# Score matmuls reordered in the diagonal sets, and the last full-array matmul ahead of a score phase issued in three parts

## The chip, the core and the metric

The kernel runs on one NeuronCore of one Trainium2 chip. The metric is the device time of one execution in microseconds. Five engines run side by side, each with its own instruction stream: TensorE (PE, which multiplies matrices; its weight loads are shown as a row of their own, PEld), VectorE (DVE), ScalarE (ACT), GpSimd (POOL) and SyncE (SP, which issues DMAs). They wait for each other through semaphores.

## What is computed

Four blocks follow one another on a 2048x512 input in bf16, each after a layer norm and with a residual: A, B, A, B. Block A is attention with 32 heads of 16 dimensions in four segments of 512 tokens, with a causal softmax inside a segment and a linear memory of the segments before. Block B is linear attention.

```python
def _A_ref(x, wq, wk, wv, wo, beta):
    ...
    for s in range(N):
        qs, ks, vs = (q[:, :, s].copy(), k[:, :, s].copy(), v[:, :, s].copy())
        logits = jnp.einsum('bhqd,bhkd->bhqk', qs, ks) * scale + mask
        p = _softmax(logits, axis=-1)
        a_dot = jnp.einsum('bhqk,bhkd->bhqd', p, vs)
        pq = phi(qs)
        num = jnp.einsum('bhld,bhde->bhle', pq, M)
        den = jnp.einsum('bhld,bhd->bhl', pq, z)[..., None] + 1e-06
        a_mem = num / den
        o = g * a_mem + (1.0 - g) * a_dot
        ...
x = A_x
x = x + _A_ref(_layernorm(x, axis=-1), A_wq, A_wk, A_wv, A_wo, A_beta)
x = x + _B_ref(_layernorm(x, axis=-1), B_wqkv, B_w_phi, B_wo)
x = x + _A_ref(_layernorm(x, axis=-1), A_wq, A_wk, A_wv, A_wo, A_beta)
x = x + _B_ref(_layernorm(x, axis=-1), B_wqkv, B_w_phi, B_wo)
```

## The kernel before

All weights and the residual stream X stay in SBUF. The kernel first records every operation of the program as an object (`Op`), with its engine, what it reads and writes, and for PE the list of its matmuls (`op.mms`: pairs of a function that gives the operands, and a number of columns). Four long tables of numbers, found beforehand, then fix everything that a scheduler would decide: `ORDER` is the order of the operations (a negative number is a filler of matmuls on zeros, an operation named "idle"; a number over 10000 is a mate, below), and others give the engine of an operation that several could run and the buffers. `finalize` works out the semaphore waits and emits each engine's instructions in that order. The tables are the same before and after.

Most of PE's work uses the whole array: 128 rows of contraction by 128 columns of weights. These are the projections (256 moving columns for K and V of block A, 512 for the output projections and for block B, 128 for the queries of A), the products of probabilities and values (17 columns each, one set of weights each), and the small products of the linear attentions. They are called full matmuls below.

The scores of block A are different. A head has only 16 dimensions, and a pair of heads fills 32 rows, so a score matmul uses one of four row groups of the array. An operation named "score" (made in `a_att`) holds the matmuls of two row groups, a = 2y and 2y + 1, for y = 0 or 1, and fills two PSUM banks (1024 columns), on which one ACT instruction then takes the exponential (`PT<-PS`, 128x1024). Three such bank pairs exist; a score operation waits until the exponential that used its pair before has read it. Where `ORDER` says so, the operations of y = 0 and y = 1 are mates: their matmuls are issued in turn, two of one and two of the other, so that all four row groups are used. A stretch of score matmuls between full ones is called a score phase.

There are two kinds of score sets. Off the diagonal, all matmuls of a set have the same 128 or 256 columns. A diagonal set has two blocks on the diagonal and one block under it: for each diagonal block two matmuls of 64 columns with the weights KP and four with the weights K, then for the block under it two of 128 columns with K. That makes 14 matmuls, the 128-column ones last, and there are 128 such operations in the program. Each matmul has its own weight load.

A PE operation without a mate is emitted by one line of `finalize`, which calls the operation's own `emit`: a loop over `op.mms` that calls `matmul`, and the semaphore is counted up by the last of them.

Of the kernel before, what the change touches and what calls it, by code (L numbers as in the profile page):

```python
# [275 lines left out]
class Program:  # L276
# [134 lines left out]
    def finalize(self, block, n_dma=40):  # L411
        nc, ops = self.nc, self.ops
        esem = {e: nc.alloc_semaphore(f"tk_{e}") for e in COMPUTE}
        dsem = [nc.alloc_semaphore(f"dma{i}") for i in range(n_dma)]
        for e in COMPUTE:
            for k, i in enumerate(x for x in self.queues[e] if not ops[x].isdma):
                ops[i].sem, ops[i].tick = ("e", e), k + 1
        q = self.queues["pool"]
        for a, b in zip(q, q[1:]):
            if ops[a].alone or ops[b].alone:  # L420
                ops[b].need.add(a)
        used = [0] * n_dma
        last = [None] * n_dma
        k = 0
        start_order = sorted((o for o in ops if o.isdma), key=lambda o: (o.done, o.i))
        for o in start_order:
            s = k % n_dma
            k += 1
            if last[s] is not None:
                o.need.add(last[s])  # L430
            last[s] = o.i
            used[s] += 16
            o.sem, o.tick = ("d", s), used[s]
        n_waits = {e: 0 for e in ENGS}
        state = {e: {} for e in ENGS}
        plan = {e: [] for e in ENGS}
        pos = {e: 0 for e in ENGS}
        clock = {}
        left = sum(len(q) for q in self.queues.values())
        while left:  # L440
            moved = False
            for e in ENGS:
                q = self.queues[e]
                while pos[e] < len(q):
                    op = ops[q[pos[e]]]
                    if any(x not in clock for x in op.need):
                        break
                    st = state[e]
                    want = {}
                    for x in op.need:  # L450
                        o = ops[x]
                        if e == "pe" and o.sem == ("e", "pe"):
                            continue
                        if want.get(o.sem, (0, None))[0] < o.tick:
                            want[o.sem] = (o.tick, x)
                    waits = []
                    for sem, (v, x) in sorted(want.items(), key=lambda kv: -clock_size(clock, kv[1][1])):
                        if st.get(sem, 0) >= v:
                            continue
                        waits.append((sem, v))  # L460
                        for s2, v2 in clock[x].items():
                            if st.get(s2, 0) < v2:
                                st[s2] = v2
                    n_waits[e] += len(waits)
                    mine = dict(st)
                    mine[op.sem] = max(mine.get(op.sem, 0), op.tick)
                    if e == "pe":
                        st[op.sem] = op.tick
                    clock[op.i] = mine
                    plan[e].append((waits, op))  # L470
                    pos[e] += 1
                    left -= 1
                    moved = True
            assert moved, "the order of the queues has a cycle"
        sec = {"sp": block.sync, "pe": block.tensor, "act": block.scalar, "dve": block.vector, "pool": block.gpsimd}
        obj = lambda s: esem[s[1]] if s[0] == "e" else dsem[s[1]]
        finals = [(("d", s), used[s]) for s in range(n_dma) if used[s]]
        for e in ENGS:
            def body(eng, e=e):
                beside, bare = None, e == "act"  # L480
                for waits, op in plan[e]:
                    if bare and not op.isdma:
                        eng.preload_act_table_set("natural_log_exp_and_others")
                        bare = False
                    for sem, v in waits:
                        eng.wait_ge(obj(sem), v)
                    if op is beside:
                        continue
                    beside = op.mate
                    if beside is None:  # L490
                        ins = op.emit[e](eng)
                        ins.then_inc(obj(op.sem), 16 if op.isdma else 1)
                        continue
                    lag = max(0, len(op.mms) - len(beside.mms))
                    for k in range(0, lag + len(beside.mms), 2):
                        for o, k0 in ((op, k), (beside, k - lag)):
                            for f in o.mms[max(0, k0):max(0, k0 + 2)]:
                                ins = matmul(eng, f)
                                if f is o.mms[-1]:
                                    ins.then_inc(obj(o.sem), 1)  # L500
                if e == "sp":
                    for sem, v in finals:
                        if state["sp"].get(sem, 0) < v:
                            eng.wait_ge(obj(sem), v)
            sec[e](body)
        self.n_waits = n_waits
        self.plan = plan
# [6 lines left out]
def clock_size(clock, x):  # L514
    return sum(clock[x].values())


def matmul(e, f):
    o, l, r, st, sp = f[0]()
    return e.matmul(o, l, r, start=st, stop=sp, tile_position=(basep(l), basep(o)))  # L520


def basep(ap):
    st = ap.ap[0][0]
    return int(ap.offset) // int(st) if st else 0
# [14 lines left out]
class Kernel:  # L540
# [10 lines left out]
    def pe(self, mms, reads, writes, pre=(), lat=0.2, cost=None, rows=0, name="", mode=0):  # L551

        def emit(e):
            for f in mms:
                ins = matmul(e, f)
            return ins
        if cost is None:
            cost = sum(mm_cost(f[1]) for f in mms)
        op = self.P.add("pe", emit, cost, reads, writes, lat=lat, pre=pre, name=name)
        op.weight = min(1.0, sum(f[1] for f in mms) * 0.000417 / cost)  # L560
        op.mode, op.rows, op.mms = int(rows > 0), rows, mms
        return op
# [471 lines left out]
    def a_att(self, s, tss, seg, AM, starts, ends, done, by_pe=()):  # L1034
# [12 lines left out]
        o = {}  # L1047
# [3 lines left out]
        def strip(a, par, g, j):  # L1051
            return K.ap[32 * a:32 * a + 32, par, g, j * 128:(j + 1) * 128]

        def both(a, g, j):
            return seg["KP"][j].ap[32 * a:32 * a + 32, g, :]

        for n, unit in enumerate(units):
# [20 lines left out]
            for y, pt in enumerate(pts):  # L1078
                P.pri = at(ts, n + 0.5 * y)
                st = self.PS.tile("st")  # L1080
                mms, reads = [], []

                def put(left, item, q, c, m, y=y, st=st):
                    qt = QT[q // 256]
                    for b in range(2):
                        def f(a=2 * y + b, b=b):
                            x = st.slot[b] * 512 + c * 64
                            return (self.ps[:, x:x + m], left(a), qt.ap[32 * a:32 * a + 32, item[1], q % 256:q % 256 + m], True, True)
                        mms.append((f, m // 4))
                for item, off in zip(unit, offs):  # L1090
                    g = item[1]
                    if item[0] == "S":
                        par, j, qs = item[2:]
                        reads += [K((par, j)), K((par, j, 1)), K(("both", j))] + [QT[i // 2](i % 2) for i in qs]
                        put(lambda a, par=par, g=g, j=j: strip(a, par, g, j), item, qs[0] * 128, off, 128 * len(qs))
                    else:
                        i = item[2]
                        reads += [K((1, i)), K((0, i)), K((1, i, 1)), K(("both", i)), seg["KP"][i](), QT[i // 2](i % 2)]
                        put(lambda a, g=g, i=i: both(a, g, i), item, i * 128, off, 64)
                        for par in range(2):  # L1100
                            put(lambda a, par=par, g=g, i=i: strip(a, par, g, i), item, i * 128 + 64, 6 + off // 4 if par else off + 1, 64)
                op = self.pe(mms, reads, [st()], pre=[pt], lat=0.23, cost=0.23, rows=y + 1, name="score")
                op.place = (self.L, s, n)
                self.act(lambda e, st=st, pt=pt: e.activation(  # L1104
# [9 lines left out]
            for ts in tss:  # L1114
                for g in range(NG):
# [7 lines left out]
                    for a in range(4):  # L1123
                        mms, used = [], []
# [351 lines left out]
```

## Time and profile before

| | us |
|---|---|
| median of 3 runs | 479.1 |
| lowest and highest of them | 478.38, 481.18 |
| the profiled execution, its own time | 478.63 |
| span of the profiled execution, first to last instruction | 476.9 |
| PE busy in the span | 465.2 |
| ACT busy | 429.7 |
| DVE busy | 424.0 |
| POOL busy | 268.9 |

The granted TensorE clock was 1.000 over the whole span. The time beside the span, 478.63 - 476.9 = 1.7 us, is start and end of the execution. A busy time sums the records of an engine without their overlaps. The end of a matmul's record is modelled, and lies some 0.17 us behind the point from which the next matmul can start, so that PE's busy share says little. What matters for PE is the distance from one matmul's start to the next one's start, which the timeline shows to 0.01 us. In a row of the timeline, the first number is the start, the second the time from there to the end of the last record in the group, and "x4" the number of instructions merged into the row.

### The profile page before, as it was taken

What the parts mean: (1) busy time and instruction counts of PE and PEld (TensorE: products, weight loads), DVE (VectorE), ACT (ScalarE), POOL (GpSimd) and SP (SyncE); (2) the same over time, 40 slices, a digit from 0 to 9 for tenths busy, and PEclk for the clock granted to TensorE, in tenths of its full rate; (3) what the DMA queues carried; (4) which work ended last, traced back from release to release, by engine and by line L of the source; (5) the groups of instructions that cost most, each with busy time, mean ns of one, the idle gap of its engine ahead of it and who ended that gap; (6) DMA issues with size and microseconds to landing.
All of it is one profiled execution on the core that took longest, in us unless ns stands there. A gap on an engine that the chain in (4) does not pass through costs nothing.

```text
span 476.9 us, 19206 instructions
## 1 busy us (share of the span) xinstructions
PE 465.2 (98%) x8309; PEld 319.3 (67%) x8309; DVE 424.0 (89%) x1008; ACT 429.7 (90%) x666; POOL 268.9 (56%) x435
## 2 busy tenths in 40 slices
PE   7999999999999999999999999999999999999997
PEld 6786677567756567557687666766765666665763
DVE  6999899989998988688999999999998888978885
ACT  3989999999999999986799899989999999999742
POOL 3686758656756685510267575784677578761100
DMA  8679661342422132320346417155434121313366
GB/s 264 115 202 147 144 92 25 69 69 47 48 46 47 25 65 51 36 55 4 67 62 97 74 21 134 25 75 83 59 63 63 25 47 33 51 38 58 70 128 186
DMA packets 115091, 35.86 MB, mean 75 GB/s; under 512 B 106816, under 2 KB 115008, under 8 KB 115008
## 3 DMA queue, kind: packets, MB, share of 16 engines
q1 hardware_dynamic: 112608, 32.54, 38.3%
q10 hardware_dynamic: 2400, 2.11, 1.4%
q8 instruction: 65, 1.06, 0.9%
q14 instruction: 18, 0.15, 0.1%
HBM read 6.32 MB, written 2.10 MB: 18 GB/s over the span
## 4 chain that ended last, share of the span: by engine, by line
PE 59%; DVE 18%; ACT 17%; DMA 3%; POOL 2%; issue 1%; POOLq 0%; DVEq 0%
PE PS L520 57%; ACT PT L1104 12%; DVE D L1110 2%; DVE stats L801 2%; DVE Vt L1228 2%; ACT Ek L1200 2%; DVE xn L817 1%; PE PS L601 1%; DMA EQ<-xn 1%; PE PS L1431 1%; DMA OT<-O 1%; DVE O L1139 1%; ACT K L1285 1%; DVE X L1165 1%; DVE Zk L1209 1%
## 5 line engine op out<-in xcount | busy, mean ns | idle before, releaser
L1104 ACT ACTIVATE PT<-PS 128x1024 bf16<-128x1024 f32 x288 | 284.6, 1083 | 7.8 <-PE PS L520 7.5
L1110 POOL TENSOR_TENSOR D<-PT,modd 128x256 bf16<-128x256 bf16 x133 | 91.6, 699 | 54.2 <-ACT PT L1104 39.1
L1113 POOL TENSOR_SCALAR_AFFINE_SELECT PT<-PT 128x512 bf16<-128x512 bf16 x128 | 83.9, 664 | 30.8 <-DVE D L1110 27.4
L520 PEld LDWEIGHTS PS<-VT,PT 128*128 128x128 bf16 x2048 | 75.0, 96 | 19.2 <-POOL PT L1113 2.5
L520 PE MATMUL PS<-VT,PT 128*128 128x17 bf16 x2048 | 82.4, 171 | 0.7 <-POOL PT L1113 0.2
L520 PE MATMUL PS<-QT,K 32*128 32x64 bf16 (+2 forms) x2176 | 77.9, 213 | 0.3
L520 PE MATMUL PS<-VT,D 128*128 128x17 bf16 x512 | 59.9, 170 | 0.0
L520 PEld LDWEIGHTS PS<-QT,K 32*128 32x128 bf16 x2176 | 41.5, 93 | 20.6 <-ACT PT L1104 10.5
L1110 DVE TENSOR_TENSOR D<-PT,modd 128x256 bf16<-128x256 bf16 x123 | 42.9, 362 | 2.9 <-ACT PT L1104 1.5
L520 PEld LDWEIGHTS PS<-VT,D 128*128 128x128 bf16 x512 | 43.2, 96 | 0.0
L1228 DVE TENSOR_TENSOR Vt<-PS,Zk 128x1024 bf16<-128x1024 f32 (+1 forms) x34 | 39.0, 1158 | 2.0 <-PE PS L520 1.0
L801 DVE BATCH_NORM_STATS2 stats<-X 128x6 f32<-128x512 bf16 x56 | 37.3, 681 | 2.5 <-DMA X<-in_A_x_dram 2.2
L1200 ACT ACTIVATE Ek<-PS 128x512 bf16<-128x512 f32 x64 | 37.6, 664 | 0.9 <-PE PS L520 0.9
L520 PE MATMUL PS<-WA_v,xA 128*128 128x256 bf16 x256 | 36.6, 273 | 0.1
L520 PE MATMUL PS<-WA_k,xA 128*128 128x256 bf16 x256 | 36.3, 273 | 0.2 <-POOL xA L907 0.2
L520 PE MATMUL PS<-xA,WA_q 128*128 128x128 bf16 x512 | 35.7, 219 | 0.5 <-DVE MS L986 0.2
L1165 DVE TENSOR_TENSOR X<-X,PS 128x512 bf16<-128x512 bf16 x50 | 33.7, 679 | 2.2 <-PE PS L520 1.8
L1207 POOL TENSOR_TENSOR Vt<-Ek 128x512 f32<-128x512 bf16 x24 | 27.9, 1164 | 12.9 <-ACT Ek L1200 10.4
L520 PEld LDWEIGHTS PS<-xA,WA_q 128*128 128x128 bf16 x512 | 29.8, 98 | 4.6 <-issue 0.6
L520 PE MATMUL PS<-WA_o,OT 128*128 128x512 bf16 x128 | 32.0, 380 | 0.6 <-DMA OT<-O 0.4
L520 PE MATMUL PS<-WB_o,OT 128*128 128x512 bf16 x128 | 32.1, 379 | 0.1
L1304 POOL COPY O<-rho 128x512 bf16<-128x512 bf16 x24 | 14.9, 634 | 26.5 <-DVE rho L1297 23.3
(157 smaller groups left out, 980.7 us busy)
## 6 DMA issues: line engine op xcount, KB each, us to landing
X<-in_A_x_dram SPq DMA_DIRECT2D x3, 512.0 KB, 9.9
EQ<-in_B_wqkv_dram SPq DMA_DIRECT2D x2, 512.0 KB, 5.4
out_dram<-X SPq DMA_DIRECT2D x8, 128.0 KB, 2.0
out_dram<-X ACTq DMA_DIRECT2D x8, 128.0 KB, 1.9
OT<-O SPq DMA_TRANSPOSE x42, 3.2
WB_v<-in_B_wqkv_dram SPq DMA_DIRECT2D x1, 512.0 KB, 4.3
WA_o<-in_A_wo_dram SPq DMA_DIRECT2D x1, 512.0 KB, 6.5
WB_o<-in_B_wo_dram SPq DMA_DIRECT2D x1, 512.0 KB, 4.7
```

Source lines behind the costliest of these rows:

```text
L520: return e.matmul(o, l, r, start=st, stop=sp, tile_position=(basep(l), basep(o)))
L601: ins = e.transpose(self.bank(gen).bitcast(BF16)[:, dt * 128:(dt + 1) * 128], src()[:, dt * 128:(dt + 1) * 128], self.ident[:])
L801: self.dve(lambda e, t=t, src=src: e.bn_stats(self.stats[:, t, :], src()), 0.603, [held() if held else R("X", t)], [R("stats", t)], name=" ...
L817: self.dve(lambda e, t=t, n=n, xn=xn: e.tensor_scalar(xn.ap[:, n], self.X[:, t, :], self.mv[:, t, 0:1], self.rstd[:, t:t + 1], op0=ALU.sub ...
L1104: self.act(lambda e, st=st, pt=pt: e.activation(pt.ap[:].rearrange("p b c -> p (b c)"), self.ps[:, st.slot[0] * 512:st.slot[0] * 512 + 102 ...
L1110: self.either(lambda e, d=d, k=k, pt=pt: e.tensor_tensor(d.ap[:, :, k, :].rearrange("p b (z c) -> p b z c", z=2), self.ends(pt.ap[:, :, 25 ...
L1113: self.pool(lambda e, q=quarters: e.affine_select(q(), q(), [[0, 4], [1, 128]], ALU.is_ge, 0.0, base=0, channel_multiplier=-1), 0.6, [pt() ...
L1165: self.dve(lambda e: e.tensor_tensor(X[:, t, :], X[:, t, :], self.bank(gen), ALU.add), 0.6, [R("X", t), gen()], [R("X", t)], name="resid")
L1200: self.act(lambda e, sgn=sgn, Ek=Ek, gen=gen: e.activation(Ek.ap[:, sgn, :], self.bank(gen), ACT.Exp, scale=1.0 - 2.0 * sgn), 512, [gen()] ...
L1207: self.pool(lambda e, Ek=Ek, sums=sums: e.tensor_tensor(sums(), *(Ek.ap[:].rearrange("p s (h j) -> p s h j", h=H)[:, :, :, 8 * k:8 * k + 8 ...
L1228: self.dve(lambda e, w=w, n=n, Vt=Vt, Zk=Zk, gen2=gen2: e.tensor_tensor(self.signed(Vt)[:, w, :, 0:16], self.bank(gen2).rearrange("p (h d) ...
L1304: P.add(("act", "pool"), {"act": lambda e, dst=dst, src=src: e.activation(dst(), src(), ACT.Copy), "pool": lambda e, dst=dst, src=src: e.t ...
```

## The change

The change has two parts. In `a_att`, the matmuls of a score operation are sorted by their columns, the widest first (the sort is stable). Sets off the diagonal stay as they are; in a diagonal set the two matmuls of 128 columns now come first. In `finalize`, the operation that follows on the same engine is looked up. Where PE's next operation is a score operation and the present one is a plain operation whose last matmul has at least 256 columns, that last matmul is issued as three: the first half of the columns, then a quarter, then a quarter, all with the same weights, and the third counts up the semaphore.

```diff
-                for waits, op in plan[e]:
+                for (waits, op), follow in zip(plan[e], plan[e][1:] + [(None, None)]):
...
                     if beside is None:
-                        ins = op.emit[e](eng)
+                        if follow[1] is not None and e == "pe" and follow[1].name == "score" and op.mms and op.name != "idle" and op.mms[-1][1] >= 256:
+                            for f in op.mms[:-1]:
+                                matmul(eng, f)
+                            ins = in_parts(eng, op.mms[-1])
+                        else:
+                            ins = op.emit[e](eng)
                         ins.then_inc(obj(op.sem), 16 if op.isdma else 1)
                         continue
...
+def in_parts(e, f):
+    o, l, r, st, sp = f[0]()
+    n, m = o.shape[1], r.shape[1]
+    for a, b in ((0, 2), (2, 3), (3, 4)):
+        ins = e.matmul(o[:, n * a // 4:n * b // 4], l, r[:, m * a // 4:m * b // 4], start=st, stop=sp and b == 4, tile_position=(basep(l), basep(o)))
+    return ins
...
                             put(lambda a, par=par, g=g, i=i: strip(a, par, g, i), item, i * 128 + 64, 6 + off // 4 if par else off + 1, 64)
+                mms.sort(key=lambda m: -m[1])
                 op = self.pe(mms, reads, [st()], pre=[pt], lat=0.23, cost=0.23, rows=y + 1, name="score")
```

In the whole program 81 full matmuls are divided: 38 of 256 columns (into 128, 64 and 64) and 43 of 512 columns (into 256, 128 and 128). PE's matmuls go from 8309 to 8471, 162 more, with 162 more weight loads. No other engine's instructions change, nor do the waits.

The next two lists show PE in the first layer, at about 155 to 157 us of the span: four matmuls of block B's value projection (`WB_v,xB`), a diagonal score operation alone, two matmuls of block B's query projection (`EQ,WB_q`), and another diagonal score operation. First before:

```order
L520 MATMUL PS<-WB_v,xB 128x512 x4
L520 MATMUL PS<-QT,KP 128x64 x2
L520 MATMUL PS<-QT,K 128x64 x4
L520 MATMUL PS<-QT,KP 128x64 x2
L520 MATMUL PS<-QT,K 128x64 x4
L520 MATMUL PS<-QT,K 128x128 x2
L520 MATMUL PS<-EQ,WB_q 128x512 x2
```

And with the change:

```order
L525 MATMUL PS<-WB_v,xB 128x512 x3
L532 MATMUL PS<-WB_v,xB 128x256
L532 MATMUL PS<-WB_v,xB 128x128 x2
L525 MATMUL PS<-QT,K 128x128 x2
L525 MATMUL PS<-QT,KP 128x64 x2
L525 MATMUL PS<-QT,K 128x64 x4
L525 MATMUL PS<-QT,KP 128x64 x2
L525 MATMUL PS<-QT,K 128x64 x4
L525 MATMUL PS<-EQ,WB_q 128x512
L532 MATMUL PS<-EQ,WB_q 128x256
L532 MATMUL PS<-EQ,WB_q 128x128 x2
```

The fourth `WB_v` matmul and the second `EQ,WB_q` matmul became three each, and the pair of 128 columns moved from the end of the score phase to its beginning.

The same for a last matmul of 256 columns, at about 14 us: four matmuls of the key projection (`WA_k,xA`), then two diagonal score operations that are mates. Before:

```order
L520 MATMUL PS<-WA_k,xA 128x256 x4
L520 MATMUL PS<-QT,KP 128x64 x4
L520 MATMUL PS<-QT,K 128x64 x8
L520 MATMUL PS<-QT,KP 128x64 x4
L520 MATMUL PS<-QT,K 128x64 x8
L520 MATMUL PS<-QT,K 128x128 x4
```

With the change:

```order
L525 MATMUL PS<-WA_k,xA 128x256 x3
L532 MATMUL PS<-WA_k,xA 128x128
L532 MATMUL PS<-WA_k,xA 128x64 x2
L525 MATMUL PS<-QT,K 128x128 x4
L525 MATMUL PS<-QT,KP 128x64 x4
L525 MATMUL PS<-QT,K 128x64 x8
L525 MATMUL PS<-QT,KP 128x64 x4
L525 MATMUL PS<-QT,K 128x64 x8
```

Here the fourth `WA_k` matmul became one of 128 and two of 64 columns, and the four 128-column score matmuls moved ahead of the 24 of 64 columns.

## The prediction

> **What bounds the kernel now.** I read the page first, then the windows, then the timeline of PE around score phases. The page's span, PE line and chain:
>
> ```profile
> span 476.9 us, 19206 instructions
> PE 465.2 (98%) x8309; PEld 319.3 (67%) x8309; DVE 424.0 (89%) x1008; ACT 429.7 (90%) x666; POOL 268.9 (56%) x435
> PE 59%; DVE 18%; ACT 17%; DMA 3%; POOL 2%; issue 1%; POOLq 0%; DVEq 0%
> PE PS L520 57%; ACT PT L1104 12%; DVE D L1110 2%; DVE stats L801 2%; DVE Vt L1228 2%; ACT Ek L1200 2%; DVE xn L817 1%; PE PS L601 1%; DMA EQ<-xn 1%; PE PS L1431 1%; DMA OT<-O 1%; DVE O L1139 1%; ACT K L1285 1%; DVE X L1165 1%; DVE Zk L1209 1%
> ```
>
> The chain that ended last runs through PE for 59% of the span, 57% of it line 520, the line that issues every matmul the change touches. ACT's exponential (L1104) has 12%. The windows show that this holds through the middle of the program (PE busy is the third number, then PEld, DVE, ACT, POOL and the granted clock), and the waits what the weight loader is held by most:
>
> ```profile
> 120.00:240.00 120.00, 118.43 (x2053) 78.24 (x2051) 104.62 (x245) 109.25 (x186) 58.12 (x92) 1.00 0.26 44
> 240.00:360.00 120.00, 119.18 (x2336) 85.78 (x2335) 114.84 (x287) 113.95 (x151) 79.70 (x126) 1.00 0.45 71
> PEld PS L520 <- ACT PT L1104: 22.0, 68, 0.6
> ```
>
> PE is hardly ever empty, and the clock is full. So a nanosecond more or less between two matmuls counts for between 0.57 of itself (the chain's share) and all of it. The next rows give matmuls and loads of each width, grouped:
>
> ```profile
> L520 PE MATMUL PS<-VT,PT 128*128 128x17 bf16 x2048 | 82.4, 171 | 0.7 <-POOL PT L1113 0.2 <-DVE VT L737 0.2
> L520 PE MATMUL PS<-WA_k,xA 128*128 128x256 bf16 x256 | 36.3, 273 | 0.2 <-POOL xA L907 0.2
> L520 PE MATMUL PS<-xA,WA_q 128*128 128x128 bf16 x512 | 35.7, 219 | 0.5 <-DVE MS L986 0.2 <-DVE X L1165 0.2
> L520 PE MATMUL PS<-WA_o,OT 128*128 128x512 bf16 x128 | 32.0, 380 | 0.6 <-DMA OT<-O 0.4 <-DVE Vt L1228 0.2
> L520 PEld LDWEIGHTS PS<-VT,PT 128*128 128x128 bf16 x2048 | 75.0, 96 | 19.2 <-POOL PT L1113 2.5 <-issue 2.3 <-ACT PT L1104 1.9
> ```
>
> The second number behind the bar is the record of one: 171 ns at 17 columns, 219 at 128, 273 at 256, 380 at 512. Most of it overlaps the next matmul. The distance from start to start follows from timeline rows with a run of equal matmuls, as (length of the row minus one record) over (count minus 1):
>
> ```profile
> 179.83 1.90 PE L520 MATMUL PS<-WA_o,OT 128*128 128x512 bf16 x8
> 54.12 1.05 PE L520 MATMUL PS<-WA_k,xA 128*128 128x256 bf16 x8
> 99.50 0.55 PE L520 MATMUL PS<-xA,WA_q 128*128 128x128 bf16 x7
> 182.42 0.27 PE L520 MATMUL PS<-VT,PT 128*128 128x17 bf16 x5
> ```
>
> For 512 columns (1.90 - 0.380) / 7 = 0.217 us, for 256 (1.05 - 0.273) / 7 = 0.111, for 128 (0.55 - 0.219) / 6 = 0.055, for 17 (0.27 - 0.171) / 4 = 0.025. From 256 to 512 columns it grows by 0.106, so a column takes 0.414 ns: 0.212, 0.106, 0.053 and 0.007 us of streaming. On top come 0.002 to 0.005 us a matmul for the wide ones and 0.018 for 17 columns.
>
> **The switches.** Around score phases PE loses more. These rows show six score phases (`QT,K` and `QT,KP`), with what comes ahead of them or the first full matmul behind:
>
> ```profile
> 182.54 0.17 PE L520 MATMUL PS<-VT,D 128*128 128x17 bf16 x1
> 182.65 0.40 PE L520 MATMUL PS<-QT,K 32*128 32x128 bf16 x16
> 182.98 0.29 PE L520 MATMUL PS<-Vt,Ek 128*128 128x136 bf16 x2
> ...
> 99.98 0.40 PE L520 MATMUL PS<-QT,K 32*128 32x256 bf16 x8
> ...
> 155.14 1.02 PE L520 MATMUL PS<-WB_v,xB 128*128 128x512 bf16 x4
> 156.09 0.20 PE L520 MATMUL PS<-QT,KP 32*128 32x64 bf16 x2
> ...
> 156.43 0.60 PE L520 MATMUL PS<-EQ,WB_q 128*128 128x512 bf16 x2
> 156.97 0.20 PE L520 MATMUL PS<-QT,KP 32*128 32x64 bf16 x2
> ...
> 13.77 0.61 PE L520 MATMUL PS<-WA_k,xA 128*128 128x256 bf16 x4
> 14.31 0.21 PE L520 MATMUL PS<-QT,KP 32*128 32x64 bf16 x4
> 14.35 0.23 PE L520 MATMUL PS<-QT,K 32*128 32x64 bf16 x8
> 14.41 0.20 PE L520 MATMUL PS<-QT,KP 32*128 32x64 bf16 x4
> 14.44 0.28 PE L520 MATMUL PS<-QT,K 32*128 32x64 bf16 x12
> 14.65 0.28 PE L520 MATMUL PS<-WA_v,xA 128*128 128x256 bf16 x1
> ...
> 152.37 0.39 PE L520 MATMUL PS<-QT,K 32*128 32x256 bf16 x4
> 152.69 0.39 PE L520 MATMUL PS<-WB_k,xB 128*128 128x512 bf16 x1
> ```
>
> The time from the end of the last full matmul's streaming to the first score matmul is: behind 17 columns 0.11 - 0.007 = 0.10 us; behind 128 columns, with the run of seven from 99.50 to 99.98, 0.48 - 6 x 0.055 - 0.053 = 0.10; behind 512 columns 0.95 - 3 x 0.217 - 0.212 = 0.09, and at 156.43 0.54 - 0.217 - 0.212 = 0.11; behind 256 columns 0.54 - 3 x 0.111 - 0.106 = 0.10. It is one figure, whatever the width of the last matmul. The first score matmul had 64, 128 or 256 columns in these rows, which makes no difference either.
>
> **Part 1, the last full matmul in three.** It removes 81 matmuls and adds 243. Per division of 512 columns: 0.111 + 2 x 0.055 - 0.217 = 0.004 us. Per division of 256: one of 128 and two of 64 columns. A full matmul of 64 columns stands nowhere in this trace; its streaming is 0.0265, and the part on top lies between the 0.002 of 128 columns and the 0.018 of 17. I take 0.003, because four score matmuls of 64 columns that run side by side, with four loads, come at 0.03 (14.35 to 14.41 is two rounds). That makes 0.055 + 2 x 0.0295 - 0.111, or 0.003; since two matmuls more cost twice what stands on top, I use 0.005 for either kind: 81 x 0.005 = 0.4 us more. At the upper end, with 0.018, a division of 256 costs 0.055 + 2 x 0.0445 - 0.111 = 0.033, in all 38 x 0.033 + 43 x 0.005 = 1.5 us. At the lower end the switch behind a narrow part is shorter than read by the scatter of these readings, 0.02: 81 x 0.02 = 1.6 us less.
>
> The weights of the added parts are loaded again, 162 times, at 0.096 us a record. I cost that at nothing: the 17-column matmuls each bring their own load of the same 128 x 128 and follow each other at 0.025 us, so such a load is hidden behind the matmuls ahead of it even where these are narrow.
>
> Against this stands a rule of the Trainium skill, TensorE: Matmul & The Clock Gate, Part 3, "The mechanism": a weight load overlaps matmuls in flight only where their row groups differ. A full matmul fills all row groups, so by that rule each added load would be exposed, an estimate of 162 x 0.096 = 15.6 us; the 0.025 us of the 17-column rows does not agree with it for full matmuls that follow one another, while a load for a score matmul behind a full one does behave so.
>
> **Part 2, the widest score matmuls first.** No instruction is added. In a score phase the time from first start to the next full matmul is 0.32 us for two rounds of 256 columns (152.37), 0.33 for four of 128 (182.65), 0.34 for the diagonal one of six rounds of 64 and one of 128 (14.31). Each holds 512 columns for every row group, 0.212 us; the rest is 0.11, 0.12 and 0.13, about 0.004 for each round more. A diagonal set has seven rounds in either order, and the way out costs the same behind 128 and behind 256 columns. So I take 0. Behind a last round of 64 columns no row shows it; the bound is one step of these three, 0.01 us to either side, times some 100 diagonal phases (128 operations, part of them mates): 1.0 us less or more. The semaphores still count up behind the last matmul of each operation, so no exponential starts earlier or later than by these nanoseconds, and nothing is queued behind a new wait.
>
> **The sum** is 0.4 us on PE, of which 0.57 to 1.0 reaches the end: 0.3. The profiled execution took 478.63, so it would take 478.9; the median of the runs shown is 479.1, so I forecast 479.4. With the bounds of both parts, -2.6 us at 0.57 and +2.5 in full, the forecast's own range is 477.6 to 481.6.
>
> **Rivals.** *The added loads are exposed because the parts are short (slower).* This takes a load that can hide only behind the one matmul ahead. A part of 64 columns streams for 0.0265 us, one of 128 for 0.053, one of 256 for 0.106; a load of 0.096 would stick out by 0.043 behind 128 columns and 0.070 behind 64. In a division of 256 both later loads and the next would pay: the second part 0.043, the third 0.070; of 512 only the third, 0.043. Sum 38 x 0.113 + 43 x 0.043 = 6.2 us, 3.5 to 6.2 at the end, so 482.6 to 485.3. It decides from 0.03 us a division (2.4 / 81). For it speaks only the record's length, against it the 0.025. Chance 0.22, with 0.03 of it for no overlap at all.
>
> *The switch becomes shorter (faster).* The way into a score phase costs 0.10 us, 81 times 8.1 us. If the loads of the first score matmuls may start once only a short last part is in the array, half of it might go: 4.0 - 0.4 = 3.6 us less, 475.5. It decides from 0.035 us a switch. Against it: 0.10 behind 17 columns as behind 512. For it: no row has a last matmul with the same weights as the one ahead. Chance 0.22.
>
> *The change meets PE while it waits anyway.* Where the loader waits for the exponential (68 times, 22.0 us), the added nanoseconds vanish: then the time stays at 479.1. Chance 0.12.
>
> **The numbers.** The forecast has 0.44. About 0.5%, 2.4 us, is what a measurement of this kernel can tell from no change. The forecast and the third rival lie within it: same 0.56, faster 0.22, slower 0.22. The range takes in the faster rival and the lower end of the slower one: 475.0 to 483.0.
>
> **What would show it.** Right: start to start 0.03 us for the 64-column parts and 0.055 for those of 128; the step from the last part to the score phase at 0.09 to 0.11 behind its streaming; 0.34 from a diagonal phase's start to the next full matmul. Wrong: a step into the score phase under 0.07, parts over 0.06 at 64 columns, or a diagonal phase that is more than 0.01 from 0.34.

## The result, and the profile after

| | before | after |
|---|---|---|
| median of 20 runs, us | 478.87 | 481.75 |
| lowest and highest | 478.04, 481.18 | 479.86, 484.5 |
| ratio, with its 95% interval | | 1.0062 (1.0052 to 1.0073) |
| profiled execution and its span | 478.63, 476.9 | 481.51, 478.7 |

The change made the kernel slower by 0.6%, 2.9 us. The page of the changed kernel, its head, the instruction queue and the chain:

```profile
span 478.7 us, 19530 instructions
PE 466.8 (98%) x8471; PEld 336.5 (70%) x8471; DVE 422.8 (88%) x1008; ACT 430.1 (90%) x666; POOL 268.0 (56%) x435
q8 instruction: 66, 1.08, 1.0%
PE PS L525 53%; ACT PT L1118 13%; DMA OT<-O 5%; ACT Ek L1214 2%; PE PS L532 2%; DVE stats L814 2%; DVE Vt L1242 2%; DMA X<-in_A_x_dram 1%; DVE D L1124 1%; PE PS L614 1%; PE PS L1445 1%; DVE O L1153 1%; DVE xn L830 1%; ACT K L1299 1%; DVE O L1356 1%
```

Two things differ from before. The transposing DMA of the attention output (`OT<-O`) went from 1% of the chain to 5%, though no DMA was touched. And the queue q8, which brings instructions, has 66 packets where it had 65:

```profile
q8 instruction: 65, 1.06, 0.9%
```

The two profiled executions differ by 2.9 us, but their spans by 1.8 only. The time beside the span went from 1.7 to 2.8 us, and the trace of the changed kernel has one more instruction packet, 1.8 us behind the last instruction (DMA view of 478.7 to 482 us):

```profile
q8 instruction: 1, 0.02, 2.4%
```

The kernel before has no packet there. In the 83 further executions of it on record the time beside the span is 1.7 to 1.8 us; in 8 of the 20 of the changed kernel it is 1.9 to 2.8. The only other trace below with such a late packet (64 instructions more, kernel before) is the only other one with over 1.8 us beside the span. That the end waits for this packet is argued from this coincidence. It is not the whole loss, since the median span is 480.0 us in the changed kernel against 477.0 before; the profiled execution, with 478.7, is one of the shorter ones, and its trace shows only a part of the usual loss.

The place that the prediction worked out, in the timeline of the changed kernel (columns: start, length, group; "x3" in line 532 is the divided matmul):

```profile
155.43 0.81 PE L525 MATMUL PS<-WB_v,xB 128*128 128x512 bf16 x3
156.07 0.38 PE L532 MATMUL PS<-WB_v,xB 128*128 128x256 bf16 x3
156.39 0.23 PE L525 MATMUL PS<-QT,K 32*128 32x128 bf16 x2
...
156.73 0.39 PE L525 MATMUL PS<-EQ,WB_q 128*128 128x512 bf16 x1
156.95 0.38 PE L532 MATMUL PS<-EQ,WB_q 128*128 128x256 bf16 x3
157.27 0.23 PE L525 MATMUL PS<-QT,K 32*128 32x128 bf16 x2
```

From the first `WB_v` matmul to the score phase it is 0.96 us (before 0.95), from `EQ,WB_q` to the next one 0.54 (before 0.54), and the diagonal phase between them takes 0.34 (before 0.34). Over all sites, the median time from the start of the last full matmul, or of its first part, to the first score matmul went from 205 to 210 ns (38 of 256 columns) and from 311 to 316 ns (43 of 512). That is 0.005 us a site, 0.4 us in all. So the two edits cost nothing that could be 2.9 us where they stand.

The time is lost elsewhere. The waits of PE for the transpose `OT<-O` (total, times, longest), before:

```profile
PE PS L520 <- DMA OT<-O: 0.4, 1, 0.4
```

and after:

```profile
PE PS L525 <- DMA OT<-O: 1.9, 4, 0.7
```

One of the four places is at 137 us. Before, the output projection `WA_o,OT` follows the last probability product at once:

```profile
137.53 0.17 PE L520 MATMUL PS<-VT,D 128*128 128x17 bf16 x1
137.55 1.02 PE L520 MATMUL PS<-WA_o,OT 128*128 128x512 bf16 x4
```

With the change PE stands there:

```profile
137.39 0.17 PE L525 MATMUL PS<-VT,D 128*128 128x17 bf16 x1
137.84 0.81 PE L525 MATMUL PS<-WA_o,OT 128*128 128x512 bf16 x3 [0.28 <-DMA OT<-O]
```

PE arrived 0.14 us earlier than before and left 0.29 us later. The transpose was not issued later: SyncE started it at 133.04 us before and at 132.95 after. It took longer. The DMA view of 132.5 to 136.5 us, before:

```profile
q1 hardware_dynamic: 1761, 0.44, 58.2%
issues: line engine op xcount, KB each, median us to landing
OT<-O SPq DMA_TRANSPOSE x1, 3.2
K<-ktok SPq DMA_TRANSPOSE x1, 3.1
```

and after:

```profile
q1 hardware_dynamic: 1559, 0.39, 95.3%
q8 instruction: 1, 0.02, 1.7%
issues: line engine op xcount, KB each, median us to landing
OT<-O SPq DMA_TRANSPOSE x1, 4.8
K<-ktok SPq DMA_TRANSPOSE x1, 4.3
```

An instruction packet lies in the window now, and both transposes in flight landed 1.2 to 1.6 us later. The packets of q8 are 16 KB. PE has 8309 matmuls and as many weight loads, 16,618 instructions, and 65 packets: 256 instructions a packet, and counted in the trace PE works off 255 instructions on average between one packet's start and the next one's (157 to 356). So q8 is read as PE's own instruction stream. It adds up over the run: of the 100 transposes, those with a q8 packet running between 1.2 and 3.2 us after their issue landed after 4.08 us on average before (42 of them) and 4.08 after (43), the others after 3.22 (58) and 3.23 (57). It is no strict rule: of the 36 that landed later than 3.6 us in the changed kernel, called late below, 29 met such a packet and 7 did not. But it holds in all fourteen traces of this document, with means of 3.8 to 4.2 us against 3.2 to 3.3, and it is not that some transposes are slow by themselves. The transposes are the same 100 in every kernel, and 94 of them landed at least twice with such a packet and twice without; in 93 of the 94 the mean with the packet is the later one, by 0.8 us on average. In the changed kernel about as many are met as before, but others: of its 36 late ones, 20 were late before as well.

The theory is therefore this. The 162 added matmuls and their loads are 324 instructions, 1.3 packets, spread over the program. They move each later fetch against the transposes, and the order of the kernel happens to suit the old places of the fetches better than the new ones. These places, against the transposes, are called the phase of the fetches. The rivals: the added instructions cost time by their number, the parts cost it by standing ahead of a score phase, or the sort costs it.

### The profile page after: what moved, and what is told of

It reads as the page before. It is cut to its first block, busy times and chain, and to the rows that moved or that the text cites. A ratio compares the mean times of both kernels' runs of the same rounds, so it can differ in the third digit from the quotient of the medians.

```text
span 478.7 us, 19530 instructions
## 1 busy us (share of the span) xinstructions
PE 466.8 (98%) x8471; PEld 336.5 (70%) x8471; DVE 422.8 (88%) x1008; ACT 430.1 (90%) x666; POOL 268.0 (56%) x435
## 4 chain that ended last, share of the span: by engine, by line
PE 57%; ACT 18%; DVE 15%; DMA 7%; POOL 1%; issue 1%; ACTq 0%; POOLq 0%; DVEq 0%
PE PS L525 53%; ACT PT L1118 13%; DMA OT<-O 5%; ACT Ek L1214 2%; PE PS L532 2%; DVE stats L814 2%; DVE Vt L1242 2%; DMA X<-in_A_x_dram 1%; DVE D L1124 1%; PE PS L614 1%; PE PS L1445 1%; DVE O L1153 1%; DVE xn L830 1%; ACT K L1299 1%; DVE O L1356 1%
## 5 line engine op out<-in xcount | busy, mean ns | idle before, releaser
L525 PE MATMUL PS<-QT,K 32*128 32x128 bf16 (+2 forms) x2176 | 81.1, 214 | 1.2 <-ACT PT L1118 0.2
L525 PEld LDWEIGHTS PS<-QT,K 32*128 32x128 bf16 x2176 | 45.5, 93 | 18.3 <-ACT PT L1118 3.1
L525 PE MATMUL PS<-WA_v,xA 128*128 128x256 bf16 x236 | 34.4, 273 | 0.1
L525 PE MATMUL PS<-WA_k,xA 128*128 128x256 bf16 x238 | 34.4, 274 | 0.2 <-POOL xA L920 0.2
L525 PE MATMUL PS<-WA_o,OT 128*128 128x512 bf16 x117 | 29.6, 380 | 1.0 <-DMA OT<-O 1.0
```

## Experiments, one part of the change at a time

All ratios are against the kernel before, on the same chip.

**The sort alone.** The line `mms.sort(key=lambda m: -m[1])` is put into the kernel before.

> Only the order of the score matmuls in the diagonal sets is changed; nothing is divided. Three theories of the 2.9 us. Number: the 162 added matmuls and loads cost it through what PE has to be supplied with, wherever they stand. Place: the parts cost it because they stand right ahead of a score phase. Sort: the widest-first order costs it. Number and place both expect this kernel within 0.3 us of before (478.9); sort expects about 481.3, that is 2.4 us more.

Measured: 478.68 us, ratio 1.000 (0.9989 to 1.0012). The sort costs nothing, and its theory falls. This kernel has as many instructions at each place as the one before.

**The parts alone.**

```diff
-                mms.sort(key=lambda m: -m[1])
```

> Only the last full matmul ahead of a score phase is issued in three parts; the score matmuls keep their old order. Number and place both expect about 481.5 (2.4 to 2.9 us more than before). Sort expects 0.4 us more than before, the direct cost of 81 divisions at 0.005 us.

Measured: 481.84 us, 1.0055 (1.0036 to 1.0075). The whole loss comes with the parts.

**Two halves, without the sort.**

```diff
-    for a, b in ((0, 2), (2, 3), (3, 4)):
+    for a, b in ((0, 2), (2, 4)):
```

> Parts alone, but two halves instead of a half and two quarters: 81 matmuls and loads are added, not 162. Number expects half of the cost of the three parts, 1.2 to 1.5 us more than before. Place expects nearly all of it where a divided matmul as such disturbs the score phase, or none where the small size of the last part does. Sort expects 0.2 us more.

Measured: 478.26 us, 0.9993 (0.9983 to 1.0003). Half of the added instructions cost nothing at all, which number does not explain.

**The same parts elsewhere, without the sort.** 38 of the 90 matmuls of 256 columns and 43 of the 212 of 512 columns that end an operation with no score operation behind it, evenly spread:

```diff
-if follow[1] is not None and e == "pe" and follow[1].name == "score" and op.mms and op.name != "idle" and op.mms[-1][1] >= 256:
+if e == "pe" and apart(op, follow[1]):
...
+def apart(op, follow):
+    if follow is None or follow.name == "score" or not op.mms or op.name == "idle" or op.mms[-1][1] < 256:
+        return False
+    w = op.mms[-1][1]
+    SEEN[w] += 1
+    return any(SEEN[w] == 1 + k * EACH[w] // MOST[w] for k in range(MOST[w]))
```

> The same number of divisions, 38 of 256 columns and 43 of 512 into a half and two quarters, but at operations that no score operation follows, spread evenly over the program; the score matmuls keep their old order. Number expects the same as with the parts ahead of score phases, 2.4 to 2.9 us more than before. Place and sort expect the direct cost alone, 0.4 us more.

Measured: 480.67 us, 1.0038 (1.0024 to 1.0053). That is 1.9 us more, less than the 2.4 to 2.9 that number gave and far more than the 0.4 of place alone. So place falls as well. The count of instructions runs much as in the changed kernel here, and 30 of the 35 late transposes are those that are late there.

## Experiments, the same work with the fetches moved

These leave all real matmuls as they are and lengthen the instruction stream only. At its start the kernel issues 25 filler matmuls on zeros while PE waits for its first data. They are replaced by more and narrower ones of about the same columns; the numbers are given with each.

```diff
+            n, w = (153, 20) if n == 25 else (n, 120)
             for _ in range(n):
-                ins = e.matmul(self.ps[:, b * 512 + 272:b * 512 + 512], self.warm[:], self.warm[:, None, 0:120].to_broadcast([128, 2, 120]), start=True, stop=True)
+                ins = e.matmul(self.ps[:, b * 512 + 272:b * 512 + 272 + 2 * w], self.warm[:], self.warm[:, None, 0:w].to_broadcast([128, 2, w]), start=True, stop=True)
```

**Before, a whole packet more (256 instructions).**

> The kernel before, with the 25 filler matmuls of 240 columns at its start replaced by 153 of 40 columns: 256 PE instructions more (matmuls and weight loads), as many as one 16 KB block of instructions that a DMA fetches for PE, and the same columns, while PE waits for data anyway. No matmul of the real work changes. Theory fetch phase: the time depends on where the block fetches, about 65 in the run, fall against the transposing DMAs, since a transpose with a fetch in its flight lands about 0.9 us later. A whole block leaves every later fetch where it was: within 0.15% of before (478.7), and the same transposes are late. Theory number: more PE instructions cost time as such, so 256 more cost about as much as the 324 of the change: 2.0 to 2.5 us more. Theory parts: the divided matmuls themselves cost it: no change.

Measured: 478.37 us, 0.9996 (0.9987 to 1.0005). In the DMA view of 133.5 to 137.5 us there is no instruction packet, and the transpose lands as before:

```profile
q1 hardware_dynamic: 2095, 0.52, 67.6%
issues: line engine op xcount, KB each, median us to landing
OT<-O SPq DMA_TRANSPOSE x1, 3.2
K<-ktok SPq DMA_TRANSPOSE x1, 3.1
```

**Before, half a packet more (128 instructions; 89 fillers, 34 in place of 20).**

> The same, with 89 fillers of 68 columns: 128 PE instructions more, half a block. Fetch phase: every later fetch moves by half a block, some 3.5 us, other transposes are late than before, and the time leaves that of before by more than 0.2%, more likely up, since the order of the kernel before was found with the old phase; the kernel with a whole block more does not leave it. Number: half of what 256 cost, 1.0 to 1.3 us more. Parts: no change.

Measured: 481.3 us, 1.0059 (1.0035 to 1.0083), the size of the loss under study, with no matmul of the work changed and with fewer instructions than the kernel that lost nothing. The view of 134.7 to 139.5 us:

```profile
q1 hardware_dynamic: 2112, 0.52, 97.8%
q8 instruction: 1, 0.02, 1.2%
issues: line engine op xcount, KB each, median us to landing
OT<-O SPq DMA_TRANSPOSE x1, 4.9
K<-ktok SPq DMA_TRANSPOSE x1, 4.3
```

and PE behind it, in the timeline:

```profile
138.79 0.17 PE L520 MATMUL PS<-VT,D 128*128 128x17 bf16 x1
139.59 0.59 PE L520 MATMUL PS<-WA_o,OT 128*128 128x512 bf16 x2 [0.63 <-DMA OT<-O]
```

It is the same transpose and the same wait as in the changed kernel, with 0.63 us in place of 0.28. Of the 30 late transposes only 5 are late in the kernel before; with the whole packet 27 of 32 are. Number falls here: 256 instructions cost nothing, 128 cost 2.6 us.

**The changed kernel, 208 and 64 instructions more (129 fillers with 24, 57 with 53).**

> The changed kernel whole, with 129 fillers of 48 columns at its start: 208 PE instructions more, so that each later fetch falls about 48 instructions later than in the changed kernel, counted to the next block. In the profile of the changed kernel the fetches at 135.6, 293.3, 321.5 and 457.4 us lie by about 1 us too early for the transposes for which PE waits there. Fetch phase: part of the loss comes back, 0.3 to 2 us less than the changed kernel, so 479.5 to 481.4 with before at 478.7. Number: 532 instructions more than before, 3.5 to 4.5 us more than before. Parts: the same as the changed kernel, about 481.5.

> The changed kernel whole, with 57 fillers of 106 columns at its start: 64 PE instructions more; each later fetch falls about 1.7 us earlier than in the changed kernel. Fetch phase: another set of late transposes than with 208 more; at the sites named the fetches begin while the transposes are still being started, so no more than 0.5 us comes back: 481.0 to 482. Number: 388 instructions more than before, 2.9 to 3.5 us more than before. Parts: the same as the changed kernel, about 481.5.

Measured: 480.99 us, 1.0047 (1.0035 to 1.006), and 479.76 us, 1.0021 (1.0013 to 1.003). The first came out inside its bounds, the second did not: 2.0 us of the 2.9 came back, where 0.5 at most was expected. PE's waits for `OT<-O` are 0.5 us in one place in that second kernel.

In the first, with 208, no wait of PE stands under the name `OT<-O`, and yet it is 2.2 us behind the kernel before. Its waits for transposes stand under other names. The timeline, and the DMA view of 292 to 297.6 us:

```profile
297.51 0.81 PE L525 MATMUL PS<-WB_o,OT 128*128 128x512 bf16 x3 [0.84 <-DVE mv L815]
q8 instruction: 1, 0.02, 1.9%
OT<-O SPq DMA_TRANSPOSE x1, 5.2
```

This matmul starts 0.35 us after that transpose landed, just as the two that wait for `OT<-O` by name in the kernel with 128 above (118.26 and 139.59 us). Three more start 0.35 us behind a transpose into a tile that they read, after waits of 0.78, 0.67 and 0.68 us (24.81, 51.48 and 103.47 us). So the waits that are listed for `OT<-O` are less than what PE waits for transposes.

That the time moves with the phase is confirmed; which phase is good cannot be read off by moving the fetches past a few transposes, since the others move as well.

**The remaining points of the two curves.**

> The kernel before with 57 fillers of 106 columns at its start: 64 PE instructions more, a quarter of a fetched block. Fetch phase: a time of its own between 478 and 482, another set of late transposes than with none, 128 or 256 more. That is one point of a curve over one block, of which 0, 128 and 256 instructions gave 1.000, 1.006 and 1.000 of before. Number: 0.5 to 0.7 us more.

> The kernel before with 121 fillers of 50 columns at its start: 192 PE instructions more, three quarters of a block. Fetch phase: the last point of the curve, between 478 and 482. With the points at 0, 64 and 128 it gives the mean of the kernel before over all phases. Number: 1.5 to 2 us more, and more than with 128.

> The changed kernel whole with 89 fillers of 68 columns at its start: 128 PE instructions more. With 0, 64 and 208 more (481.75, 479.76 and 480.99 us) it gives the mean of the changed kernel over the phases. If all of its loss but the direct cost of the parts is phase, this mean lies 0 to 1 us above the mean of the kernel before over its phases; if the change cost 2.5 us in itself, the mean lies about 2.5 us above. This point itself: between 479 and 482.

Measured: 479.25 us, 1.0010 (1.0001 to 1.0019); 482.52 us, 1.0080 (1.0050 to 1.0109); 482.89 us, 1.0088 (1.0054 to 1.0123). The last two lie above the 482 us that was their upper bound.

The granted clock has a part in this. In 3 of 6 executions with 192, in 5 of 9 of the changed kernel with 128, and in 2 of 10 of the kernel before with 128, the mean clock was 0.986 to 0.993. In the other executions it was 0.999 or 1.000, and their medians are 481.0, 480.3 and 480.8 us: still a loss, but of 1.6 to 2.2 us (the last section shows such a fall).

| instructions more at the start | before | changed |
|---|---|---|
| 0 | 1 | 1.0062 |
| 64 | 1.0010 | 1.0021 |
| 128 | 1.0059 | 1.0088 |
| 192 (before), 208 (changed) | 1.0080 | 1.0047 |
| 256 | 0.9996 | not run |
| mean of the first four | 1.0037 | 1.0054 |

The means differ by 0.0017, 0.8 us. Combined from the intervals of the seven ratios, each taken as independent, that is uncertain by some 0.0014, or 0.2 to 1.5 us for the change itself. This takes in the noise of the runs alone. Four points that scatter by 0.8%, one of them not at the same place in both, are a coarse mean, and a cost of nothing is not ruled out. The sites themselves show 0.4 us. So the larger part of the 2.9 us is read as the phase in which the change left the fetches, since 2.0 us of it came back with the same work and 64 more instructions at the start.

**Two halves without the sort, 128 instructions more (89 fillers).**

> The kernel with the last full matmul ahead of a score phase in two halves, which took 478.26 us, now with 89 fillers of 68 columns at its start: 128 PE instructions more. Fetch phase: its equal time was a lucky phase and leaves 478.3 by more than 0.2%, most likely upwards, 479.5 to 481.5. If halves as such are harmless where three parts are not, it stays within 0.15% of 478.3.

Measured: 480.6 us, 1.0059 (1.0033 to 1.0084). The halves were at no loss by their phase, not by being halves. Part of this is the clock again: it was 0.989 to 0.993 in 5 of the 12 executions, and the median of the other seven is 479.7 us, 1.4 above the halves without fillers. The number of late transposes does not order the kernels: in the traces this one has the fewest, 21, and the halves without fillers the most, 38.

No kernel that was run is faster than the one before beyond its interval; the nearest are the halves (0.9993) and the whole packet (0.9996).

## Why the prediction was right and wrong

**The price of the parts held.** Divided matmuls follow one another as worked out: 0.38 us for the three at 156.07, less the last one's record of 0.219, is 0.16 from the first to the third start, against 0.111 + 0.055 = 0.166. Two parts of 64 columns, which the trace before did not have, start 0.028 us apart (median of 38), against the 0.0295 assumed; their row shows a record of 193 ns and no idle time:

```profile
L532 PE MATMUL PS<-WA_v,xA 128*128 128x64 bf16 x40 | 4.4, 193 | 0.0
```

**The switch held.** The way into a score phase costs 0.1 us behind narrow parts too, so the faster rival has nothing to show. The added loads stay hidden, against the rule of the Trainium skill that was weighed (TensorE: Matmul & The Clock Gate, Part 3, "The mechanism"): the site at 155.43 is 0.01 us longer, where two exposed loads of 0.096 would add 0.19. So the slower rival was wrong in its mechanism, although the time went its way. (Its own sum comes to 6.1 us, not 6.2.)

**The sort held** at 0: 0.34 us a phase, and 1.000 when run alone.

**What failed is the sum.** It took 0.4 us on PE, "of which 0.57 to 1.0 reaches the end", as all that the change does; the 162 loads were costed "at nothing" because the array hides them. Neither step looked at the instructions as something that must be fetched. The page showed q8 with 65 packets, and a division by PE's instruction count would have shown that 324 more are 1.3 packets. The waits for `OT<-O` are 1.9 us after against 0.4 before, 1.5 us more, and the spans of the two profiled executions differ by 1.8. The two do not match place by place: by the starts of ACT's 666 instructions, which are the same in both, the changed kernel is 0.9 us behind at 84 us, level at 132 and 1.8 behind at the end. So some of the waits are taken up on the way, and the rest is not assigned. The forecast of 479.4 lay 2.35 us too low, and "within 0.5%" was the wrong side to favour; the intervals here tell 0.1% apart.

That 481.75 lies inside the stated range is luck. The forecast's own sum ended at 481.6, with parts of 64 columns at a price that they did not have, and the range went on to 483.0 only for exposed loads, which did not happen.

**The third rival**, that PE's own waits take up the cost so that the time stays, is refuted by the time.

What stays open: the link from a fetch to a late transpose rests on the traces, where the same transposes are late with a fetch and not without, and on the moved fetches, not on a transpose measured alone. Why the fetch holds up the transposes was not tried, and which late transposes delay the end of the program, and which do not, was not worked out.

## What to carry to other kernels

A change that adds or removes instructions moves every later instruction fetch, and in a kernel whose order is fixed beforehand, that alone can cost more than the change: here 0.6 to 0.8% for 128 or 192 filler instructions at the start, a part of it by the clock, and nothing for 256. Before judging an edit of a few tenths of a per cent, run it with some fillers of a fraction of a fetched packet, and compare means over the phases. Where the time moves and no row around the edit does, look at the DMAs that the bounding engine waits for, also where a wait is put down to an engine that was done, and at what shares their window.

## What was not expected of the hardware

Behind a late transpose the clock fell in some executions. In the kernel before with 192 instructions more, PE stood for 1.13 us at 44 us, ahead of a matmul that waits for a transpose (the row names an engine that was done; in the kernel before, it is `OT<-EQ` with 0.28 us):

```profile
43.80 0.27 PE L520 MATMUL PS<-WA_k,xA 128*128 128x256 bf16 x1
45.20 0.38 PE L520 MATMUL PS<-O,OT 128*128 128x128 bf16 x4 [1.13 <-DVE PhiK L949]
```

In the windows behind it (PE busy first, the granted clock third from the end) the clock falls to half for some 7 us:

```profile
44.00:46.00 2.00, 0.87 (x29) 0.80 (x30) 1.34 (x5) 1.63 (x3) 0.34 (x2) 1.00 0.33 70
46.00:48.00 2.00, 2.00 (x32) 1.12 (x28) 2.00 (x5) 1.69 (x2) 0.59 (x1) 0.80 0.94 182
48.00:50.00 2.00, 2.00 (x39) 1.25 (x39) 1.61 (x4) 1.60 (x3) 1.97 (x4) 0.50 0.48 89
50.00:52.00 2.00, 2.00 (x29) 1.21 (x27) 1.12 (x5) 1.28 (x3) 0.22 (x1) 0.50 0.00 0
52.00:54.00 2.00, 2.00 (x6) 0.60 (x4) 1.97 (x10) 1.21 (x2) 1.09 (x2) 0.50 0.00 0
54.00:56.00 2.00, 2.00 (x29) 0.97 (x28) 0.04 (x1) 2.00 (x4) 1.13 (x2) 0.99 0.98 189
```

That execution was 0.8 us behind the kernel before at the end of the wait and 3.4 us behind at 54 us, when the clock was full again. The halves with 128 instructions more show the same at the same place, behind a wait of 1.41 us: their mean granted clock is 0.989, that of this kernel 0.992.

But the wait alone does not bring the fall. In the changed kernel with 128 instructions more, PE stood longer at the same place, and the clock stayed full:

```profile
45.97 0.38 PE L525 MATMUL PS<-O,OT 128*128 128x128 bf16 x4 [1.27 <-DMA OT<-EQ]
46.00:48.00 2.00, 2.00 (x46) 1.59 (x47) 1.61 (x3) 1.18 (x3) 0.00 (x0) 1.00 0.72 140
48.00:50.00 2.00, 2.00 (x53) 1.53 (x51) 2.00 (x6) 2.00 (x4) 1.82 (x3) 1.00 0.72 138
```

What else it takes stays open. The Trainium skill (TensorE: Matmul & The Clock Gate, "Why this matters for your kernels") warns of gaps over about 3 us; in the trace shown a gap of 1.13 us stood ahead of the fall.
